# Tiles of an attention and two-MLP kernel made 32 bytes longer, at other places mod 128 bytes

## The chip, the cores and the metric

The kernel runs on one core of one Trainium2 chip. The metric is the time of one execution on the device in microseconds, as the median of the runs.

## The reference

Chunked attention, then an MLP with a product of two projections, then an MLP with a rational function, all in float32:

```python
batch, n_heads, seq, head_dim = (4, 8, 576, 64)      # 2304 tokens, d_model 512
# attention within chunks of 64 tokens
scores = scale * np.matmul(q_c, k_c.transpose(0, 1, 2, 4, 3))
attn = softmax(scores)                                # over the 64 keys of the chunk
x = np.matmul(attn, v_c)                              # -> [2304, 512]
# first MLP, d_ff 1536
a = x @ w_a
b = x @ w_b
y = a * b @ w_out
# second MLP, d_ff 2048
h = y @ w_in
P = a[0] + a[1] * h + a[2] * h2 + a[3] * h3           # h2 = h * h, h3 = h2 * h
Q = 1.0 + np.abs(b[0]) * np.abs(h) + np.abs(b[1]) * h2
out = (P / (Q + 1e-06)) @ w_out2
```

The weights come as float64; the kernel reads them as pairs of 32-bit words.

## The kernel before

Each float32 operand of a product is split into a high and a low part of type float32r, and a product is the sum of three matmuls: high by high, high by low, low by high (`mm3`, lines 252 to 254; for y the same three stand in lines 682, 683 and 685). Every matmul has its own load of weights.

The work runs in stages on TensorE. First, for the first 768 tokens, attention in units of 128 tokens runs interleaved with the projections a and b (`ab_half`). While this goes on, the 24 tiles of w_a and w_b arrive as raw words (`w_fetch`, line 172), are turned into float32 by ScalarE and VectorE in four pieces (`w_piece`) and split (`w_hi`, `w_lo`). Attention of the other 1536 tokens follows the same way, and its result is turned into sums of blocks of x. Second, from some 175 us, a and b of these tokens are made from seven products of such sums in place of eight (`s_product`, `s_step`). Third, from some 354 us, y is made in five blocks of tokens (`y_banks`), while the weights of the second MLP are converted. Fourth, from some 500 us, come h, the rational function and the output, in five blocks of 384, 512, 512, 512 and 384 tokens and 16 steps each (`step2`): `h_part` multiplies w_in by y, `g_front`, `g_back` and `g_split` make the function on ScalarE and VectorE, `o_part` multiplies by w_out2.

The order of the work is written out by hand, as a list for the start, as due times for attention, and as loops for the rest. The loads of q, k, v and the weights are issued by SyncE in this order.

These are the pools that the change touches. All tiles have 128 partitions.

- `p_w`: 12 tiles, w0 to w11, of 4096 bytes per partition. w0 to w7 hold w_a and w_b, high parts in the first half and low parts in the second; w8 to w11 are a ring of four for raw words (`AHEAD`). Later w0 to w11 hold w_out; some of them hold factors of the sums (`ws_`). In the fourth stage w0 to w3 hold y of even blocks, w8 to w11 y of odd blocks (`y_fetch`, one tile for each quarter of d_model), w4 to w6 the temporaries u, t and r (`h_tile`, two halves used in turn), w7 every third pair g_hi and g_lo (`g_split`).
- `p_w2`: 32 tiles, v0 to v31, of 4096 bytes, for w_in (even numbers) and w_out2 (odd numbers). It lies over the memory of the X tiles and others, which are dead by then.
- `p_X`: 14 tiles of 6144 bytes, for the sums of x (`x_block`) and, before that, for k, q and v of the first six units (`a_load`).

Other pools keep their tiles: x of the first tokens (`p_x0`), which later holds factors of the sums (`j_x`), g_hi and g_lo (`p_g`), results on the way to memory (`p_io`), the ring of |h| (`a_ring`). The lengths of all these tiles are multiples of 128 bytes.

Of the kernel before, what the change touches and what calls it, by code (L numbers as in the profile page):

```python
# [9 lines left out]
F32 = mybir.dt.float32  # L10
F32R = mybir.dt.float32r
I32 = mybir.dt.int32
# [8 lines left out]
def chunk_attention_two_mlps(  # L21
# [34 lines left out]
    nc = tc.nc  # L56
    P = 128
    B, H, S, D = q.shape
    NT, DM = out.shape
# [7 lines left out]
    F2 = DFF2 // P  # L67
# [6 lines left out]
    GH = GT // 2  # L74
    UH = GH // P
    NQ = NT // GT
# [9 lines left out]
    AHEAD = 4  # L86
    NWP = 12 - AHEAD
# [5 lines left out]
    START2 = [sum(SIZES2[:j]) for j in range(len(SIZES2))]  # L93
# [6 lines left out]
    p_w = ctx.enter_context(tc.tile_pool(name="w", bufs=1))  # L100
# [8 lines left out]
    y_d = dram.tile([P, KD, NT], F32, name="y_d", tag="y_d")  # L109
# [8 lines left out]
    def split(hi, lo, x):  # L118
        nc.scalar.copy(hi, x)
        nc.vector.tensor_tensor(lo, x, hi.bitcast(F32), ALU.subtract)  # L120
# [4 lines left out]
    p_X = s_X.enter_context(tc.tile_pool(name="X", bufs=1))  # L125
# [22 lines left out]
    w_at = {key: n for n, key in enumerate(order)}  # L148
    w1_d = {k: dram.tile([P, DM], F32, name=f"w_{k[0]}_{k[1]}", tag=f"w_{k[0]}_{k[1]}") for k in order1}

    wt = {}
    raws = {}
    terms = {}
# [4 lines left out]
    def w_fetch():  # L158
        key = order[n_cv[0]]
        at = n_cv[0]  # L160
        n_cv[0] += 1
        if at < len(order1):
            t = p_w.tile([P, DM, 2], I32, name="w_raw", tag=f"w{NWP + at % AHEAD}")
        elif at < len(order1) + len(ordero):
            t = p_x32.tile([P, DM, 2], I32, name="w_raw", tag="x32")
        else:
            t = p_cv.tile([P, DM, 2], I32, name="w_raw", tag="w_raw")
        dst = t.rearrange("p f t -> p (f t)")
        src = w_src[key]
        if len(src.shape) == 3:  # L170
            dst = dst.rearrange("p (k f) -> p k f", k=src.shape[1])
        nc.sync.dma_start(out=dst, in_=src)
        raws[key] = t

    def w_tile(key, dtype):
        at = w_at[key]
        if at < len(order1):
            pool, tag = p_w, f"w{at % NWP}"
        elif at < len(order1) + len(ordero):
            pool, tag = p_w, f"w{at - len(order1)}"  # L180
        else:
            pool, tag = p_w2, f"v{at - len(order1) - len(ordero)}"
        t = pool.tile([P, 2, DM], dtype, name=f"w_{key[0]}_{key[1]}_{at}", tag=tag)
        return t[:, 0], t[:, 1]

    def w_fetch_ahead(n):
        while n_cv[0] < n_cv[2] and n_cv[0] < n + (AHEAD if n_cv[0] < len(order1) else 2):
            w_fetch()

    def w_hi(n):  # L190
        if n in f32s:
            key = order[n]
            wt[key] = w_tile(key, F32R)
            nc.scalar.copy(wt[key][0], f32s[n].bitcast(F32))
# [6 lines left out]
    def w_piece():  # L201
# [5 lines left out]
        if piece == 0:  # L207
            w_fetch_ahead(n)
            t = raws.pop(key)

            terms[n] = (t, *w_tile(key, I32))
# [68 lines left out]
    raw = {}  # L280
    un = {}
# [5 lines left out]
    xs = {}  # L287

    def x_block(g, c):
        if (g, c) not in xs:  # L290
            xs[g, c] = p_X.tile([P, 2, 2, GH], F32R, name="xs", tag=f"X{g}_{c}")
        return xs[g, c]

    def a_tmp(u, name):
# [6 lines left out]
    def a_load(u, *names):  # L301

        (b0, c0), (b1, c1) = divmod(2 * u, NCH), divmod(2 * u + 1, NCH)
        for nm, src in (("k", k), ("q", q), ("v", v)):
            if nm not in names or u >= NU:
                continue
            if u < 2 * UH:
                if ("raw", u) not in un:
                    un["raw", u] = p_X.tile([P, 3, H, D], F32, name="kqv", tag=f"X{NQ - 1}_{u + 1}")
                t = un["raw", u][:, "kqv".index(nm)]  # L310
            else:
                t = p_qk.tile([P, H, D], F32, name=nm, tag=nm, bufs=2 if nm == "v" else 1)
            if b0 == b1:
                parts = [(t, src[b0, :, c0 * CH:(c0 + 2) * CH, :])]
            else:
                parts = [
                    (t[c * CH:(c + 1) * CH], src[bb, :, cc * CH:(cc + 1) * CH, :])
                    for c, (bb, cc) in enumerate(((b0, c0), (b1, c1)))
                ]
            for dst, s in parts:  # L320
                nc.sync.dma_start(out=dst, in_=s.rearrange("h s d -> s h d"))
            raw[nm, u] = t
# [181 lines left out]
    j_x = {}  # L504
    J_AT = {"20": 0, "21": 1, "10": 2, "11": 3, "a1": 4, "b": 5}

    def j_room(nm):

        t, at = divmod(J_AT[nm], 3)
        if ("j", t) not in j_x:  # L510
            j_x["j", t] = p_x0.tile([P, 3, 2, DM], F32R, name="j_x", tag=f"x_{('hi', 'lo')[t]}")
        return j_x["j", t][:, at]
# [8 lines left out]
    def s_prep(i):  # L521


        f = wf.pop(i)
        flat = f.rearrange("p a f -> p (a f)")
        n = 2 * P
        made = {}

        def place(nm):
            if nm == "a" and i % 2 == 0:  # L530
                return p_j2.tile([P, 2, DM], F32R, name="ws_a", tag="ws_a")

            at = {"20": 8, "10": 9, "a1": 10, "b0": 11, "b1": 11}.get(f"{nm}{i}")
            if nm == "b":
                if at not in j_x:
                    t = j_room("b") if at is None else p_w.tile([P, 2, DM], F32R, name="ws_b", tag=f"w{at}")
                    j_x[at] = t.rearrange("p a f -> p (a f)").rearrange("p (i a f) -> p i a f", i=2, a=2)
                return j_x[at][:, i % 2]
            if at:
                return p_w.tile([P, 2, DM], F32R, name="ws_" + nm, tag=f"w{at}")  # L540
            return j_room(f"{nm}{i % 2}")

        def hi(nm, at, m, products):
            def f():
                t = made[nm] = place(nm)[:, :, :m]
                for x, c in enumerate(products):
                    ws[i, c] = t[:, 0, x * n:(x + 1) * n], t[:, 1, x * n:(x + 1) * n]
                nc.scalar.copy(t[:, 0], flat[:, at:at + m])
            return f

        def lo(nm, at, m):
            return lambda: nc.vector.tensor_tensor(
                made[nm][:, 1], flat[:, at:at + m], made[nm][:, 0].bitcast(F32), ALU.subtract
            )

        def add(o, x, y, op):
            return lambda: nc.vector.tensor_tensor(f[:, o], f[:, x], f[:, y], op)

        return [
            hi("a", 0, 2 * n, (1, 2)), hi("b", 3 * n, n, (4,)), lo("a", 0, 2 * n), lo("b", 3 * n, n),  # L560
            add(3, 2, 3, ALU.add), add(2, 0, 2, ALU.subtract), add(0, 3, 0, ALU.subtract),
            hi("2", 2 * n, 2 * n, (7, 5)), add(1, 1, 0, ALU.subtract), hi("1", 0, 2 * n, (6, 3)),
            lo("2", 2 * n, 2 * n), lo("1", 0, 2 * n),
        ]
# [133 lines left out]
    y = {}  # L698

    def y_fetch(j, kk):  # L700


        n = SIZES2[j]
        t = p_w.tile([P, 2, DM], F32R, name="y", tag=f"w{kk if j % 2 == 0 else 8 + kk}")
        y[j, kk] = t[:, 0, :n], t[:, 1, :n]
        nc.sync.dma_start(out=t[:, 1, :n].bitcast(F32), in_=y_d[:, kk, START2[j]:START2[j] + n])

    def y_split(j, kk):
        hi, lo = y[j, kk]
# [13 lines left out]
    h_t = {}  # L723

    def h_tile(nm, n):

        if nm not in h_t:
            at = 4 + "utr".index(nm)
            h_t[nm] = [p_w.tile([P, 2, DM], F32, name=nm, tag=f"w{at}"), 0]
        h_t[nm][1] ^= 1  # L730
        return h_t[nm][0][:, h_t[nm][1], :n]

    def g_front(j, i):

# [20 lines left out]

    def g_split(j, i, t):
        if n_g[0] % 3 == 1:
            w = p_w.tile([P, 2, DM], F32R, name="g_hl", tag="w7")
            hi, lo = (w[:, x, :t.shape[1]] for x in range(2))
        else:  # L760
            hi, lo = (p_g.tile(t.shape, F32R, name=x, tag=x) for x in ("g_hi", "g_lo"))
        n_g[0] += 1
        split(hi, lo, t)
        g2[j, i] = (hi, lo)
# [52 lines left out]
    for item in LOADS:  # L817
        if item == "w":
            w_fetch()
        else:  # L820
            a_load(int(item[1]), item[0])
# [3 lines left out]
    for item in FIRST:  # L825
# [9 lines left out]
        what, u = item[:-1], int(item[-1])  # L835
# [40 lines left out]
    for op in range(12):  # L876
        at = min(END + 2 + 0.5 * (op // 3), 2.0 * len(seq) - 0.5)
# [30 lines left out]
    for t in range(1, F1):  # L908

        if t == 1:  # L910
            at = [(0, m // 2) for m in range(12)]
        elif t == 2:
            at = [(2, m) for m in (3, 3, 4, 5)] + [(3, m) for m in (0, 1, 2, 3, 3, 4, 5, 6)]
        else:
            at = [(2 * t - 2 + m // 6, FILLS[m % 6]) for m in range(12)]
# [19 lines left out]
    for n, (i, g) in enumerate(seq2):  # L935
        place[:] = [n, 0]
        if n == len(seq2) - 1:
# [3 lines left out]
            t = p_x32.tile([P, 2, SIZES[0]], F32, name="g_raw", tag="x32")  # L941
# [98 lines left out]
```

## Time and profile before

| | |
|---|---|
| median of 3 runs | 906.7 us (906.33 to 906.87) |
| profiled execution | 904.24 us |
| its span, first to last instruction | 902.5 us |
| busy: TensorE, its weight loads | 883.7 us (98%), 788.0 us (87%) |
| busy: VectorE, ScalarE, GpSimd | 723.3 us (80%), 612.7 us (68%), 63.9 us (7%) |
| chain that ended last | PE 92%, DVE 4%, ACT 2%, DMA 1% |
| moved by DMA | 105.83 MB |

In the rows, PE is TensorE's matmuls, PEld its weight loads, DVE VectorE, ACT ScalarE, POOL GpSimd and SP SyncE. L252 is line 252. A matmul's row in the timeline has its start and a modelled duration, which overlaps the next one; the spacing is the difference of two starts.

### The profile page before, as it was taken

What the parts mean: (1) busy time and instruction counts of PE and PEld (TensorE: products, weight loads), DVE (VectorE), ACT (ScalarE), POOL (GpSimd) and SP (SyncE); (2) the same over time, 40 slices, a digit from 0 to 9 for tenths busy, and PEclk for the clock granted to TensorE, in tenths of its full rate; (3) what the DMA queues carried; (4) which work ended last, traced back from release to release, by engine and by line L of the source; (5) the groups of instructions that cost most, each with busy time, mean ns of one, the idle gap of its engine ahead of it and who ended that gap; (6) DMA issues with size and microseconds to landing.
All of it is one profiled execution on the core that took longest, in us unless ns stands there. A gap on an engine that the chain in (4) does not pass through costs nothing.

```text
span 902.5 us, 14772 instructions
## 1 busy us (share of the span) xinstructions
PE 883.7 (98%) x5532; PEld 788.0 (87%) x5532; DVE 723.3 (80%) x1321; ACT 612.7 (68%) x1105; POOL 63.9 (7%) x122
## 2 busy tenths in 40 slices
PE   6989999999999999999999999999999999999998
PEld 5879989999999999988888998888888888888987
DVE  5657788497878886578778599998889988988886
ACT  5857888445554553678777688877677667776775
POOL 0111111111111111100000000000000000000000
PEclk9999999999999999999999999999999999999999
DMA  9969886333343423778777200200020002000100
GB/s 233 263 200 263 251 239 171 106 130 126 127 146 123 147 85 105 245 250 277 261 243 256 94 1 1 82 1 1 1 93 1 1 1 82 0 1 1 48 1 36
DMA packets 107336, 105.83 MB, mean 117 GB/s; under 512 B 61440, under 2 KB 84480, under 8 KB 107264
## 3 DMA queue, kind: packets, MB, share of 16 engines
q1 hardware_dynamic: 99264, 79.71, 29.6%
q0 software_dynamic: 8000, 25.17, 7.5%
q8 instruction: 43, 0.70, 0.3%
q14 instruction: 29, 0.24, 0.1%
HBM read 74.98 MB, written 29.88 MB: 116 GB/s over the span
## 4 chain that ended last, share of the span: by engine, by line
PE 92%; DVE 4%; ACT 2%; DMA 1%; issue 0%; SPq 0%; DVEq 0%; ACTq 0%
PE h L254 7%; PE acc L254 7%; PE acc L253 7%; PE h L252 7%; PE h L253 7%; PE acc L252 7%; PE acc L682 5%; PE acc L683 5%; PE acc L685 5%; PE ab L252 3%; PE ab L254 3%; PE ab L253 3%; PE y L253 3%; PE y L254 3%; PE y L252 3%; PE q L252 2%
## 5 line engine op out<-in xcount | busy, mean ns | idle before, releaser
L254 PE MATMUL h<-y,w_i 128*128 128x512 f32 (+1 forms) x320 | 117.8, 368 | 0.0
L252 PE MATMUL h<-y,w_i 128*128 128x512 f32 (+1 forms) x320 | 117.8, 368 | 0.0
L253 PE MATMUL h<-y,w_i 128*128 128x512 f32 (+1 forms) x320 | 117.7, 368 | 0.0
L739 ACT ACTIVATE a_ring<-h 128x512 f32<-128x512 f32 (+1 forms) x80 | 44.1, 551 | 88.0 <-PE h L254 88.0
L580 ACT COPY s<-y 128x384 f32<-128x384 f32 x72 | 34.4, 480 | 80.0 <-PE y L254 79.9
L682 PE MATMUL acc<-g_hi,w_o 128*128 128x512 f32 (+1 forms) x240 | 86.9, 369 | 0.0
L683 PE MATMUL acc<-g_hi,w_o 128*128 128x512 f32 (+1 forms) x240 | 86.8, 368 | 0.0
L742 DVE SCALAR_TENSOR_TENSOR u<-u,cb_t,a_ring 128x512 f32<-128x512 f32 (+1 forms) x80 | 55.7, 696 | 30.2 <-ACT u L740 29.4
L254 PE MATMUL acc<-w_o,g_lo 128*128 128x512 f32 x191 | 74.7, 391 | 0.0
L253 PE MATMUL acc<-w_o,g_hi 128*128 128x512 f32 x191 | 74.6, 391 | 0.0
L252 PE MATMUL acc<-w_o,g_hi 128*128 128x512 f32 x191 | 74.3, 389 | 0.0
L253 PEld LDWEIGHTS h<-y,w_i 128*128 128x128 f32 x320 | 60.1, 188 | 8.8
L252 PEld LDWEIGHTS h<-y,w_i 128*128 128x128 f32 x320 | 60.1, 188 | 8.8
L254 PEld LDWEIGHTS h<-y,w_i 128*128 128x128 f32 x320 | 60.1, 188 | 7.4
L662 DVE TENSOR_TENSOR g_lo<-g_raw,g_hi 128x512 fp32r<-128x512 f32 (+1 forms) x60 | 38.2, 638 | 28.1 <-ACT g_hi L660 15.4
L685 PE MATMUL acc<-g_lo,w_o 128*128 128x512 f32 (+1 forms) x240 | 59.3, 368 | 0.0
L741 ACT ACTIVATE t<-h,ca_t 128x512 f32<-128x512 f32 (+1 forms) x80 | 59.0, 737 | 0.0
L752 DVE SCALAR_TENSOR_TENSOR u<-u,r 128x512 f32<-128x512 f32 (+1 forms) x80 | 50.6, 632 | 9.5 <-ACT r L751 9.5
L744 DVE SCALAR_TENSOR_TENSOR t<-t,ca_t,h 128x512 f32<-128x512 f32 (+1 forms) x80 | 55.6, 695 | 2.8
L751 ACT ACTIVATE r<-r,nlsh 128x512 f32<-128x512 f32 (+1 forms) x80 | 54.5, 682 | 2.6
L750 ACT ACTIVATE r<-u,nlsh 128x512 f32<-128x512 f32 (+1 forms) x80 | 55.6, 695 | 0.3
L753 DVE SCALAR_TENSOR_TENSOR t<-t,ca_t,r 128x512 f32<-128x512 f32 (+1 forms) x80 | 55.4, 692 | 0.0
(195 smaller groups left out, 2400.9 us busy)
## 6 DMA issues: line engine op xcount, KB each, us to landing
w_raw<-in_moe_w_out_dram SPq DMA_DIRECT2D x28, 512.0 KB, 3.9
g_d<-g POOLq DMA_DIRECT2D x72, 192.0 KB, 2.5
g_raw<-g_d SPq DMA_DIRECT2D x48, 256.0 KB, 4.2
w_raw<-in_moe_w_in_dram SPq DMA_DIRECT2D x16, 512.0 KB, 4.6
w_raw<-in_moe_w_a_dram SPq DMA_DIRECT2D x12, 512.0 KB, 4.8
w_raw<-in_moe_w_b_dram SPq DMA_DIRECT2D x12, 512.0 KB, 5.2
out_dram<-o SPq DMA_DIRECT2D x18, 256.0 KB, 2.4
y_d<-ys POOLq DMA_DIRECT2D x16, 256.0 KB, 4.1
```

The lines of the kernel that those rows point to most:

```text
L252: nc.tensor.matmul(ps, wh, xh, start=first, stop=False, **kw)
L253: nc.tensor.matmul(ps, wh, xl, start=False, stop=False, **kw)
L254: nc.tensor.matmul(ps, wl, xh, start=False, stop=last, **kw)
L682: nc.tensor.matmul(acc[j][d], wh, gh, start=i == 0, stop=False)
L683: nc.tensor.matmul(acc[j][d], wl, gh, start=False, stop=False)
L685: nc.tensor.matmul(acc[j][d], cols(w, d)[0], gl, start=False, stop=i == F1 - 1)
L741: nc.scalar.activation(t, ps, AF.Identity, scale=ca_t[:, 3:4], bias=ca_t[:, 2:3])
L742: nc.vector.scalar_tensor_tensor(u, u, cb_t[:, 0:1], ah, ALU.add, ALU.mult)
L744: nc.vector.scalar_tensor_tensor(t, t, ca_t[:, 1:2], ps, ALU.add, ALU.mult)
L750: nc.scalar.activation(r, u, AF.Ln, scale=2.0 ** -LSH, bias=nlsh[:, 0:1])
L751: nc.scalar.activation(r, r, AF.Exp, scale=-1.0, bias=nlsh[:, 1:2])
L753: nc.vector.scalar_tensor_tensor(t, t, ca_t[:, 0:1], r, ALU.add, ALU.mult)
```

## The change

A helper `room` makes the tiles of the three pools 8 elements (32 bytes) longer, and hands out a part that begins 0, 4 or 8 elements (0, 16 or 32 bytes) into the tile. Tags are numbered: w0 to w11 are 0 to 11, v0 to v31 are 12 to 43, X tags get numbers from 44 on in the order of their first use. w6 to w11 begin 16 bytes in, w0 to w5 at 0. From number 12 on, four tags in a row begin at 0, the next four at 16, the next four at 32 bytes, and so on. The users of these tiles take them as flat rows and shape them themselves; what they read and write is otherwise the same.

```diff
+    def room(pool, tag, dtype, name, size=2 * DM):
+        n = rooms.setdefault(tag, len(rooms))
+        t = pool.tile([P, size + 8], dtype, name=name, tag=tag)
+        return t[:, 4 * (n > 5 if n < 12 else (n - 12) // 4 % 3):][:, :size]
+
+    rooms = {f"w{n}": n for n in range(12)}
+    rooms.update({f"v{n}": 12 + n for n in range(2 * F2)})
...
-            t = p_w.tile([P, DM, 2], I32, name="w_raw", tag=f"w{NWP + at % AHEAD}")
+            t = room(p_w, f"w{NWP + at % AHEAD}", I32, "w_raw").rearrange("p (f t) -> p f t", t=2)
...
-        t = pool.tile([P, 2, DM], dtype, name=f"w_{key[0]}_{key[1]}_{at}", tag=tag)
-        return t[:, 0], t[:, 1]
+        t = room(pool, tag, dtype, f"w_{key[0]}_{key[1]}_{at}")
+        return t[:, :DM], t[:, DM:]
...
-            xs[g, c] = p_X.tile([P, 2, 2, GH], F32R, name="xs", tag=f"X{g}_{c}")
+            t = room(p_X, f"X{g}_{c}", F32R, "xs", 4 * GH)
+            xs[g, c] = t.rearrange("p (a b f) -> p a b f", a=2, b=2)
...
-                    un["raw", u] = p_X.tile([P, 3, H, D], F32, name="kqv", tag=f"X{NQ - 1}_{u + 1}")
+                    t = room(p_X, f"X{NQ - 1}_{u + 1}", F32, "kqv", 4 * GH)
+                    un["raw", u] = t.rearrange("p (a h d) -> p a h d", a=3, h=H)
...
-                return p_w.tile([P, 2, DM], F32R, name="ws_" + nm, tag=f"w{at}")
+                return room(p_w, f"w{at}", F32R, "ws_" + nm).rearrange("p (a f) -> p a f", a=2)
...
-        t = p_w.tile([P, 2, DM], F32R, name="y", tag=f"w{kk if j % 2 == 0 else 8 + kk}")
-        y[j, kk] = t[:, 0, :n], t[:, 1, :n]
+        t = room(p_w, f"w{kk if j % 2 == 0 else 8 + kk}", F32R, "y")
+        y[j, kk] = t[:, :n], t[:, DM:DM + n]
...
-            h_t[nm] = [p_w.tile([P, 2, DM], F32, name=nm, tag=f"w{at}"), 0]
+            h_t[nm] = [room(p_w, f"w{at}", F32, nm), 0]
         h_t[nm][1] ^= 1
-        return h_t[nm][0][:, h_t[nm][1], :n]
+        return h_t[nm][0][:, h_t[nm][1] * DM:][:, :n]
...
-            w = p_w.tile([P, 2, DM], F32R, name="g_hl", tag="w7")
-            hi, lo = (w[:, x, :t.shape[1]] for x in range(2))
+            w = room(p_w, "w7", F32R, "g_hl")
+            hi, lo = (w[:, x * DM:][:, :t.shape[1]] for x in range(2))
```

The factor b of the sums (`ws_b`) in w11 goes through `room` in the same way.

## Rows read from the trace of the kernel before

**Rows 1.** The page: engines, chain by engine, DMA issues (KB, median us to landing).

```profile
PE 883.7 (98%) x5532; PEld 788.0 (87%) x5532; DVE 723.3 (80%) x1321; ACT 612.7 (68%) x1105; POOL 63.9 (7%) x122
...
PE 92%; DVE 4%; ACT 2%; DMA 1%; issue 0%; SPq 0%; DVEq 0%; ACTq 0%
...
w_raw<-in_moe_w_out_dram SPq DMA_DIRECT2D x28, 512.0 KB, 3.9
```

**Rows 2.** Stretches: from:to us, busy us (x count) of each engine, clock, DMA share, GB/s.

```profile
0.00:25.00 25.00, 16.59 (x250) 14.59 (x253) 15.29 (x39) 15.84 (x29) 1.91 (x8) 1.00 0.96 234
25.00:50.00 25.00, 20.92 (x250) 18.13 (x246) 17.90 (x43) 18.39 (x35) 3.88 (x7) 1.00 1.01 265
50.00:75.00 25.00, 23.47 (x298) 21.12 (x288) 14.84 (x35) 15.67 (x33) 3.77 (x7) 1.00 0.73 224
...
175.00:350.00 175.00, 175.00 (x1011) 174.68 (x1010) 141.34 (x276) 89.24 (x172) 25.05 (x46) 1.00 0.36 124
...
575.00:800.00 225.00, 225.00 (x994) 186.29 (x994) 200.24 (x304) 164.85 (x272) 0.00 (x0) 1.00 0.08 26
...
875.00:902.50 27.50, 23.56 (x115) 20.46 (x113) 19.00 (x36) 16.20 (x32) 0.00 (x0) 1.00 0.08 30
```

**Rows 3.** Timeline of PE, start and us: runs of 512, 384 and 256 columns.

```profile
699.72 0.39 PE L253 MATMUL h<-y,w_i 128*128 128x512 f32 x1
...
700.63 0.39 PE L254 MATMUL h<-y,w_i 128*128 128x512 f32 x1
...
224.84 0.33 PE L252 MATMUL q<-xs,j_x 128*128 128x384 f32 x1
...
225.36 0.33 PE L252 MATMUL q<-xs,j_x 128*128 128x384 f32 x1
...
371.68 0.28 PE L682 MATMUL acc<-g_hi,w_o 128*128 128x256 f32 x1
...
372.28 0.28 PE L683 MATMUL acc<-g_hi,w_o 128*128 128x256 f32 x1
```

**Rows 4.** Timeline of PE in a block of 384: first h matmuls, then the output's.

```profile
530.68 0.33 PE L252 MATMUL h<-y,w_i 128*128 128x384 f32 x1
...
531.75 0.33 PE L252 MATMUL h<-y,w_i 128*128 128x384 f32 x1
...
532.79 0.39 PE L252 MATMUL acc<-w_o,g_hi 128*128 128x512 f32 x1
...
534.87 0.33 PE L252 MATMUL h<-y,w_i 128*128 128x384 f32 x1
```

**Rows 5.** Single lines: count, duration ns min/median/max, first and last start.

```profile
L252 PEld LDWEIGHTS h<-y,w_i x320: 187/188/188, 500.5 to 889.5; 128*128 128x128 f32 x160
...
L743 DVE TENSOR_TENSOR t<-h,t x41: 682/689/692, 578.5 to 795.4; 128x512 f32<-128x512 f32 x41
...
L119 ACT CAST g_hi<-t x28: 622/627/627, 578.3 to 795.3; 128x512 fp32r<-128x512 f32 x28
...
L194 ACT CAST w_a<-w_x x12: 614/623/655, 16.0 to 157.0; 128x512 fp32r<-128x512 f32 x12
```

**Rows 6.** Chain of the head; DMA issues 25 to 50 us; tiles that change owner.

```profile
2.79 5.96 DMA kqv<-in_k_dram
...
23.97 6.14 DMA w_raw<-in_moe_w_a_dram
30.13 0.79 ACT w_a L217
...
w_raw<-in_moe_w_b_dram SPq DMA_DIRECT2D x4, 512.0 KB, 7.8
w_raw<-in_moe_w_a_dram SPq DMA_DIRECT2D x3, 512.0 KB, 8.8
...
L254 PE MATMUL q<-xs,j_x x32: 334/334/346, 301.1 to 356.2; 128*128 128x384 f32 x32
...
L221 DVE TENSOR_SCALAR w_i<-w_raw x16: 418/422/427, 366.3 to 485.7; 128x512 f32<-128x512 f32 x16
```

More of the change, by code (lines that the diff above doesn't have):

```diff
@@ L535, in place @@
                 if at not in j_x:
-                    t = j_room("b") if at is None else p_w.tile([P, 2, DM], F32R, name="ws_b", tag=f"w{at}")
-                    j_x[at] = t.rearrange("p a f -> p (a f)").rearrange("p (i a f) -> p i a f", i=2, a=2)
+                    if at is None:
+                        t = j_room("b").rearrange("p a f -> p (a f)")
+                    else:
+                        t = room(p_w, f"w{at}", F32R, "ws_b")
+                    j_x[at] = t.rearrange("p (i a f) -> p i a f", i=2, a=2)
                 return j_x[at][:, i % 2]
             if at:
-                return p_w.tile([P, 2, DM], F32R, name="ws_" + nm, tag=f"w{at}")
+                return room(p_w, f"w{at}", F32R, "ws_" + nm).rearrange("p (a f) -> p a f", a=2)
             return j_room(f"{nm}{i % 2}")
@@ L703, in y_fetch @@
         n = SIZES2[j]
-        t = p_w.tile([P, 2, DM], F32R, name="y", tag=f"w{kk if j % 2 == 0 else 8 + kk}")
-        y[j, kk] = t[:, 0, :n], t[:, 1, :n]
-        nc.sync.dma_start(out=t[:, 1, :n].bitcast(F32), in_=y_d[:, kk, START2[j]:START2[j] + n])
+        t = room(p_w, f"w{kk if j % 2 == 0 else 8 + kk}", F32R, "y")
+        y[j, kk] = t[:, :n], t[:, DM:DM + n]
+        nc.sync.dma_start(out=y[j, kk][1].bitcast(F32), in_=y_d[:, kk, START2[j]:START2[j] + n])
     def y_split(j, kk):
```

## The prediction

> **What bounds the kernel now.** I read the busy shares first. TensorE (PE) is busy 98% of the span, its weight loads (PEld) 87%, VectorE (DVE) 80%, ScalarE (ACT) 68%, and the chain that ended last consists of PE for 92% [rows 1]. The table by stretch then says where PE has no room left [rows 2]: in the stretches from 175 to 350 us and 575 to 800 us it is busy for every microsecond, at a granted clock of 1.00. Only the first 75 us (14.0 us idle) and the tail (3.9 us idle) leave anything. So an edit of operand places can move the time in three ways: the spacing of matmuls changes, the head changes, or the tail does.
>
> The spacing is read from the starts in the timeline. Four spacings of 512 columns take 0.91 us, three of 384 columns 0.52 us, five of 256 columns 0.60 us [rows 3]: 227, 173 and 120 ns. From 256 to 512 columns that is 107 ns more, 0.417 ns a column, the 2.4 GHz level. What is left over is 13.3 ns at each of the three sizes. The stretches confirm it over long times: 175 us hold 1011 matmuls, nearly all of 384 columns, and 225 us hold 994 of 512 [rows 2], 173 and 226 ns each.
>
> One irregularity exists. Where blocks of y have 384 columns, matmuls of 384 and of 512 columns alternate. There the first six of 384 take from 530.68 to 531.75, 178 ns each; the nine of 512 take from 532.79 to 534.87, 231 ns each [rows 4]. That is 0.03 and 0.04 us more than at the steady spacing, 0.07 us in a step; 32 steps (two blocks of 16) make 2.2 us.
>
> **The change part by part.** No instruction is added, removed or moved. DMAs keep their sizes, queues and order. Per partition, tiles w0 to w11, v0 to v31 and the X tiles become 32 bytes longer; each next tile of a pool then begins 32 bytes further mod 128. Before, every length in these pools is a multiple of 128 bytes, so all tiles of a pool begin at one place.
>
> *Matmul spacing.* The matmuls of lines 252 to 254 and 682 to 685 number 4128 by the loops (576 of the first product, 1008 of its sums, 720 for y, 960 for h, 864 for the output). Their 13.3 ns make 4128 x 13.3 ns = 55 us. This is the end of what could be saved, if those 13.3 ns were a collision of the moving rows and the weights, both being read from one place mod 128. I take 0, for three reasons in rows. First, the remainder is the same at 256, 384 and 512 columns and for tiles of different pools [rows 3]. Second, weight loads last 187 to 188 ns in all 320 of the h group [rows 5], without a sign of a read that sometimes meets another. Third, DVE and ACT read and write the same memory 89% and 73% of the time from 575 to 800 us [rows 2], at whatever phase they happen to have, and the matmul spacing doesn't answer. If operands at one place mod 128 hindered each other, some of these streams should show it. The 2.2 us of the irregularity is the part of the spacing that does vary; it follows a change of size, not of tile, so I leave it too, but it is the likeliest small gain. The other end is a loss: a spacing as uneven everywhere as behind a change of size, 4.4 ns (231 less 226.7) on each of 4128 matmuls, 18 us.
>
> *VectorE and ScalarE.* Line 743 on DVE, which works in place on a temporary, lasts 682 to 692 ns in 41 instances; ACT's cast of line 119 from t into g_hi lasts 622 to 627 ns [rows 5]. There is no spread here to win back. Where DMAs are dense, ACT's cast of line 194 spreads from 614 to 655 ns around 623 [rows 5], 5% at most. PE hides all of that from 75 us on. In the head, up to 50 us, the chain has 26 pieces of ACT, some 14 us; the one behind the w_raw wait is among the longer [rows 6]. 5% of them is 0.7 us either way; I take 0.
>
> *DMA.* Tiles w8 to w11 begin at 16, 48, 80 and 112 mod 128 afterwards, and w_raw of the first 24 weight tiles lands there. The kqv loads land in X tiles that keep multiples of 32. The chain shows that this matters in the head alone: 5.96 us on the first k load and 6.14 us on a w_raw load [rows 6], while the DMA engines are busy at a share of 0.96 and 1.01 [rows 2]. No row shows a landing at 16 bytes off. The nearest are loads of the same 512 KB in the same 25 us, which land in a median of 7.8 and 8.8 us [rows 6]: 1.0 us apart with nothing different in place. I take 0, since that row lies closest to what is moved. The end on the slow side: seven such loads stand in those 25 us [rows 6], some 14 in the first 50, through a ring of four tiles; 1.0 us a turn makes 14 / 4 x 1.0 = 3.5 us. The end on the fast side is the chain's load landing like the quiet ones of w_out, 3.9 us [rows 1] in place of 6.14: 2.2 us less.
> The page "DMA: Bandwidth & Descriptors" of the Trainium skill, section How a descriptor splits into AXI transactions, says that a transfer is cut at 256-byte boundaries into beats of 32 bytes and that an unaligned start costs extra beats; no run here shows it yet. By that page, an estimate: a piece of 1 KB has 32 beats and gets from one to eight more by where it begins; four more on the 7.3 MB of those loads, over half of what moves in 50 us, would be 3.7 us.
>
> *Waits for reused memory.* The v tiles lie over dead X, sum and load tiles. Their borders move by up to 1.4 KB, so a first write may have to wait for another old tile. The sums of x are read last at 356.2 us; the first piece of w_in writes at 366.3 us [rows 6]. The cover is 10 us; cost 0. Were it gone, DVE and ACT would start a piece later, and PE needs w_in only from 500 us.
>
> Sum: 0 + 0 + 0 + 0. The profiled execution took 904.24 us, of which the span is 902.5 us and 1.7 us lie around it; the median of the runs is 906.7 us, 2.5 us above. A sum of zero keeps both: 906.7 us.
>
> **The rivals.**
> (A) The 13.3 ns are a collision, and the new places undo it. For it: a remainder of the same size stands on every matmul, PE reads moving rows and the next weights at once, and the remainder isn't rigid behind a change of size [rows 4]. Against it, the three reasons above. The price follows from the places: after the change, h's weights (v0, v2, ...) and y still coincide in 10 of 64 pairs for even blocks and 6 of 64 for odd ones, about one in eight, so seven eighths of 55 us go: 48 us, 858.6 us.
> Here the skill's pages speak on both sides. "TensorE: Matmul & The Clock Gate" of the Trainium skill, section Back-to-back issue gap, has 2.5 ns over the columns for a warm matmul, where this trace has 13.3; by the page, an estimate, 4128 x 10.8 ns = 45 us of this kernel isn't the array's. "SBUF — State Buffer" of the Trainium skill, section Who interferes with whom, says that PE and ACT never wait on anyone, which is against the change.
> (B) Only small things gain: the irregularity goes, 2.2 us: 904.5 us. For it, the irregularity varies while all else is steady; against it, it looks the same for different tiles.
> (C) Slower: raw loads at 16 bytes off take longer. It happens in the first 50 us, where the DMA share is 1 and ACT waits for a w_raw at 24 us [rows 6]. It decides as soon as a load takes longer than the slack of the ring, and there is none in that stretch: 3.5 us, 910.2 us. Behind 75 us PE covers it.
> (D) New collisions: reads that kept out of each other's way meet now. 18 us: 925 us. The same rows speak against it as against A.
> If the allocator rounded the padding away, the time would be 906.7 us too; that counts with the forecast.
>
> **How the numbers follow.** Nothing that can be measured: 0.52. A 0.10, B 0.15, C 0.15, D 0.08. What a measurement can tell from no change is about 0.2%, 1.8 us; B and C lie just beyond it. So faster is 0.25, same 0.52, slower 0.23. The range takes in the forecast, B and C with the bounds of the head: down by 2.2 + 0.7 + 2.2 = 5.1 us to 901.6, rounded to 901; up by 3.5 + 0.7 us to 910.9, and with a few of D's matmuls (1.1 of its 18 us) to 912. A and D are left out, 0.18.
>
> **What would show it.** In the profile after: starts of matmuls at 512, 384 and 256 columns 227, 173 and 120 ns apart if I am right; 215 to 220, 162 to 165 and 108 to 112 if A is. Where a pair still coincides (the weights in v0 with y in w0) beside one that doesn't, A would show two spacings in one block. B shows where blocks of 384 run: the 178 and 231 ns of now would be 173 and 227. C shows in the landing of w_raw and in the idle time before 75 us, D in starts that are uneven where they are even now. I am wrong if any steady spacing moves by 1 ns: that alone is 4 us. The weakest step is that one, since no tile of before lies at another place than its neighbours.

## The result, and the profile after

| | before | after |
|---|---|---|
| median of the runs | 906.52 us (903.71 to 906.87, 4 runs) | 917.38 us (914.83 to 918.79, 4 runs) |
| profiled execution, its span | 904.24 us, 902.5 us | 916.12 us, 914.3 us |
| ratio | | 1.0124, 95% interval 1.0090 to 1.0157 |

The changed kernel is 1.24% slower, 10.9 us by the medians and 11.8 us by the two spans. The forecast of 906.7 us was wrong, and so was its range: 917.38 us lies 5.4 us above its upper end.

In the changed kernel lines 252 to 254 are 260 to 262, and 682, 683 and 685 are 695, 696 and 698. The page of the changed kernel: engines, the chain that ended last, two groups of matmuls (busy us, mean ns | idle before).

```profile
PE 894.6 (98%) x5532; PEld 789.7 (86%) x5532; DVE 723.6 (79%) x1321; ACT 612.7 (67%) x1105; POOL 64.2 (7%) x122
...
PE 93%; DVE 3%; ACT 2%; DMA 1%; SPq 1%; issue 0%; DVEq 0%; ACTq 0%
...
L260 PE MATMUL h<-y,w_i 128*128 128x512 f32 (+1 forms) x320 | 118.7, 371 | 0.0
...
L695 PE MATMUL acc<-g_hi,w_o 128*128 128x512 f32 (+1 forms) x240 | 87.8, 372 | 1.0 <-ACT g_hi L673 1.0
```

The same 5532 matmuls keep PE busy 10.9 us longer (894.6 against 883.7 in [rows 1]). DVE has 0.3 us more, ACT the same 612.7 us. So the time is on PE, and hardly in waits: the matmuls of h had no idle time in front of them, those of y 1.0 us.

The table by stretch (us, then busy us and count for each engine, granted clock, DMA share, GB/s), first of the changed kernel, then two rows of the kernel before that [rows 2] don't hold:

```profile
0.00:75.00 75.00, 60.86 (x767) 53.25 (x768) 47.73 (x113) 49.41 (x94) 9.60 (x22) 0.95 0.92 240
...
175.00:350.00 175.00, 175.00 (x1003) 174.86 (x1002) 140.39 (x274) 88.53 (x170) 25.12 (x46) 1.00 0.37 125
350.00:375.00 25.00, 23.90 (x179) 23.43 (x178) 14.11 (x31) 9.83 (x21) 2.17 (x4) 1.00 0.45 147
375.00:500.00 125.00, 125.00 (x543) 101.30 (x543) 94.12 (x173) 92.71 (x158) 8.95 (x16) 1.00 0.76 259
...
575.00:800.00 225.00, 225.00 (x974) 182.41 (x973) 196.50 (x298) 161.89 (x268) 0.00 (x0) 1.00 0.08 26
```

```profile
350.00:375.00 25.00, 24.93 (x183) 24.10 (x182) 14.98 (x32) 10.99 (x25) 2.70 (x5) 1.00 0.53 176
375.00:500.00 125.00, 125.00 (x553) 103.52 (x552) 94.47 (x173) 92.38 (x157) 8.23 (x15) 1.00 0.76 255
```

PE is busy for the whole of 575 to 800 us in both, at a granted clock of 1.00, but gets 974 matmuls done in place of 994 [rows 2]; from 375 to 500 us 543 in place of 553; from 175 to 350 us 1003 in place of 1011. The 20 lost ones are worth 20/974 x 225 = 4.6 us, the 10 are worth 2.3 us, the 8 worth 1.4 us: 8.3 us of 11.8 in three stretches, and the last stage goes on beyond 800 us. The head shows nothing of the kind: 767 matmuls and 60.9 us of PE in its 75 us, where the kernel before has 769 and 61.0 us, though the granted clock there was 0.95 in this execution and 1.00 before.

The timeline of PE in the changed kernel, 512 columns, nine spacings apart:

```profile
699.54 0.39 PE L260 MATMUL acc<-w_o,g_hi 128*128 128x512 f32 x1
...
701.64 0.39 PE L260 MATMUL h<-y,w_i 128*128 128x512 f32 x1
```

2.10 us for nine are 233 ns each, where 227 stood before [rows 3]. I took all starts of the products' matmuls from the trace and averaged the spacing by stage. "Sums" is 180 to 350 us (384 columns; a few longer gaps are in its averages), "y" 376 to 499 us, "h" and "output" 576 to 800 us (512 columns):

| ns | sums | y | h | output |
|---|---|---|---|---|
| before | 173.6 | 226.7 | 226.7 | 226.7 |
| after | 174.9 | 232.2 | 231.5 | 231.7 |

The steady spacing of before is (columns + 32) / 2.4 GHz. What lies over it adds up to 0.25 us in the sums, nothing in y and 2.0 us from 500 us on (384 and 512 columns) before, and to 1.5, 2.9 and 8.2 us after: 10.3 us more. The rest of the 11.8 us is small: one wait of 1.0 us of the first block of y for its g_hi near 350 us (in the page's row of L695, and in PE's busy time from 350 to 375 us), and some 0.4 us in the first product. That wait isn't the change's: the kernels below that are as fast as the one before have it too (1.2 us with 256 bytes, 1.0 us with the raw loads off).

### The profile page after: what moved, and what is told of

The parts are those of the page before. It is cut to its first block, busy times and chain, and to the rows that moved or that the text cites. A ratio compares the mean times of both kernels' runs of the same rounds, so it can differ in the third digit from the quotient of the medians.

```text
span 914.3 us, 14772 instructions
## 1 busy us (share of the span) xinstructions
PE 894.6 (98%) x5532; PEld 789.7 (86%) x5532; DVE 723.6 (79%) x1321; ACT 612.7 (67%) x1105; POOL 64.2 (7%) x122
## 4 chain that ended last, share of the span: by engine, by line
PE 93%; DVE 3%; ACT 2%; DMA 1%; SPq 1%; issue 0%; DVEq 0%; ACTq 0%
PE h L260 7%; PE h L261 7%; PE acc L260 7%; PE h L262 7%; PE acc L262 7%; PE acc L261 7%; PE acc L695 5%; PE acc L698 5%; PE acc L696 5%; PE ab L260 3%; PE ab L261 3%; PE ab L262 3%; PE y L261 3%; PE y L260 3%; PE y L262 3%; PE q L260 2%
## 5 line engine op out<-in xcount | busy, mean ns | idle before, releaser
L695 PE MATMUL acc<-g_hi,w_o 128*128 128x512 f32 (+1 forms) x240 | 87.8, 372 | 1.0 <-ACT g_hi L673 1.0
```

The costliest lines, as they stand in the source:

```text
L695: nc.tensor.matmul(acc[j][d], wh, gh, start=i == 0, stop=False)
```

## The experiments

Theory 1: the pace of matmuls follows from the distance of the weights being loaded from the rows being read, modulo some number of bytes; before, it supposes, every pair lies at distance 0. Its rivals: the variety of places from tile to tile does it (theory 2 of the first expectations); a place off a border of 128 bytes is slow by itself (theory 3); the traffic of other engines or the raw loads at 16 bytes off do it. "Distance" is, per partition, the place of the weights less that of the rows.

### One step of 32 or 64 bytes between pools

`pad_l`, an unused tile ahead of these pools, is made longer, which moves the w, v and X tiles together against all other pools; nothing else changes.

```diff
-    const.tile([P, 24], F32, name="pad_l", tag="pad_l")
+    const.tile([P, 32], F32, name="pad_l", tag="pad_l")
```

> Kernel before, with one unused tile at the start 32 bytes longer: w, v and X tiles all begin at 32 mod 128, the other pools (g_hi, g_lo, x of the first tokens, j_x) stay at 0. Nothing varies from tile to tile. Theory 1 (the place of the weights against the moving rows counts): y's stage, 375 to 500 us, has weights at 32 and rows at 0 and goes from 227 to about 233 ns; the output's matmuls and the first product too, the sums by 2 ns; h (both at 32) stays at 227 where it isn't behind a change. Some 10 to 13 us more than before, about 918 us. Theory 2 (it is the variety of places, since each change of tile throws the pace out as a change of size does): 906.7 us, all spacings 227 and 173 ns. Theory 3 (the place mod 128 itself counts): h gets slower as well, 920 us and more.

> As the one before, 64 bytes in place of 32. Theory 1 has two forms: if places count mod 64, as the changed kernel's trace suggests (mean spacing of 512-column matmuls 225.7 + 4.2 ns over columns both at a distance of 0 and of 64, 6 ns more at the others), this is 906.7 us with 227 ns in y's stage; if they count mod 128, about 918 us again. Theory 2: 906.7 us. Theory 3: over 910 us.

 (40 in place of 32)

Measured: 915.24 us at 32 bytes, ratio 1.0097 (1.0071 to 1.0124); 910.72 us at 64 bytes, ratio 1.0048 (1.0029 to 1.0067). The table by stretch, at 32 bytes and then at 64:

```profile
175.00:350.00 175.00, 175.00 (x995) 174.87 (x994) 139.20 (x271) 88.27 (x170) 24.55 (x45) 1.00 0.36 125
375.00:500.00 125.00, 125.00 (x548) 101.13 (x547) 94.22 (x175) 93.76 (x160) 8.90 (x16) 1.00 0.77 259
```

```profile
175.00:350.00 175.00, 175.00 (x1010) 174.80 (x1009) 140.61 (x274) 88.85 (x172) 25.08 (x46) 1.00 0.37 127
375.00:500.00 125.00, 125.00 (x545) 101.03 (x544) 94.50 (x175) 93.68 (x159) 8.89 (x16) 1.00 0.77 259
```

Spacings: at 32 bytes 176.4 ns (sums), 233.3 (y), 227.1 (h), 230.7 (output); at 64 bytes 173.6, 233.3, 226.6, 228.2. The rows from 375 us begin with up to 3 us of matmuls of 256 columns in this and the next kernels, so the spacings say more than the counts. h, whose weights (v tiles) and rows (w tiles) moved together, stays at its pace; where weights and rows moved apart, the sums, y and the output lose it at 32 bytes, y and the output at 64. That is theory 1, and against a place that is slow by itself. It isn't the variety of places either, since nothing here varies from tile to tile. One step between two pools costs nearly as much as the whole change, 9.5 of 10.9 us. A period of 64 bytes falls with the second kernel, whose 910.72 us neither form of theory 1 had expected (906.7 or 918).

The output holds a contrast within one stage. Its rows (w_out2) are in v tiles; of its weights, two thirds are in `p_g`, which stayed, and one third in w7 (g_hl), which moved with the rows. At 32 bytes, nine spacings of each:

```profile
688.61 0.39 PE L252 MATMUL acc<-w_o,g_hl 128*128 128x512 f32 x1
...
690.65 0.39 PE L252 MATMUL acc<-w_o,g_hl 128*128 128x512 f32 x1
...
694.06 0.39 PE L252 MATMUL acc<-w_o,g_hi 128*128 128x512 f32 x1
...
696.16 0.40 PE L252 MATMUL acc<-w_o,g_hi 128*128 128x512 f32 x1
```

They are 227 and 233 ns. By the starts from 576 to 800 us, the pairs that moved together have 226.7 ns at 32 and at 64 bytes, those that moved apart 232.7 and 229.0 ns.

### 128 and 256 bytes

> Kernel before, with the unused tile at the start 128 bytes longer: w, v and X tiles begin 128 bytes further than the other pools' tiles, and all tiles lie at 0 mod 128 as before. If the distance counts mod 128, as the change supposes: 906 us and 227 ns in y's stage. If it counts over a longer period, as the run of matmuls alone hints (233 ns at a distance of 128, 227 at 256): about 233 ns in y's stage and 911 to 916 us. Variety of places would say 906 us.

 (56 elements)

> As the one before with 256 bytes. If the distance counts and its period divides 256: 906 us, 227 ns in y's stage, 173 ns in the sums, like the kernel before, though every tile of three pools lies elsewhere. If not: 910 us and more.

 (88 elements)

Measured: 917.61 us at 128 bytes, ratio 1.0122 (1.0101 to 1.0142); 905.70 us at 256 bytes, ratio 0.9997 (0.9984 to 1.0010). At 128 and then at 256 bytes:

```profile
375.00:500.00 125.00, 125.00 (x547) 101.64 (x546) 94.92 (x175) 93.88 (x159) 8.85 (x16) 1.00 0.77 259
...
575.00:800.00 225.00, 225.00 (x980) 184.00 (x980) 197.93 (x300) 163.49 (x271) 0.00 (x0) 1.00 0.08 26
```

```profile
375.00:500.00 125.00, 125.00 (x554) 103.50 (x553) 94.28 (x172) 93.23 (x160) 8.77 (x16) 1.00 0.77 260
575.00:800.00 225.00, 225.00 (x994) 186.31 (x993) 200.22 (x304) 165.97 (x274) 0.00 (x0) 1.00 0.08 26
```

At 128 bytes every tile still begins at 0 mod 128, and the kernel is as slow as the changed one (spacings 175.9, 232.4, 228.8, 231.0 ns), a little slower than expected. At 256 bytes all four spacings are those of before. The period is 256 bytes, and beginning on a border of 128 bytes doesn't help. One number doesn't fit: h at 128 bytes has 228.8 ns, though its rows and weights moved together. The first seven of its twelve matmuls behind the output's are uneven, and then 227 ns is back; at 32 and 64 bytes it was there at once. Why is open.

### Matmuls alone

Three kernels of nothing but matmuls, all from the same two tiles, one for the rows and one for the weights; each run of matmuls reads both at places of its own.

```python
for r in range(count):
    m, s = places[r % len(places)]        # bytes: rows at m, weights at s
    nc.tensor.matmul(ps[:, :n], sta[:, s // 4:s // 4 + P], mov[:, m // 4:m // 4 + n], start=r == 0, stop=r == count - 1)
```

> No attention and no MLP: long runs of 40 matmuls alone, with the next weights and the moving rows at chosen places, nothing else running; its time is that of these runs. Theory 1: 512 columns at a distance of 0 (and 128, 256, 512, 1024 bytes) 226.7 ns, at 64 bytes the same or near, at 16, 32, 48, 80, 96 and 112 about 231 to 234 ns; moving rows and weights shifted together 226.7 ns. 384 columns: 173.3 at 0 and 64, 175 to 176 at the others. Theory 2: 226.7 and 173.3 ns in every run behind its first ten matmuls. Theory 3: rows and weights shifted together are slow too.

> Matmuls alone again, without attention and MLPs: each run of 36 at a chosen distance of weights and rows follows 16 at a distance of 0, so that all start from the same state. Theory of the distance with a long period: 226.7 ns at 0, 256 and 512 bytes and about 233 at 128 and 384; if it is the state left by the run before that counts, distances that came out slow in the first run of this kind come out at 226.7 here. With high and low parts in turn as in the kernels: the same as with one pair. 256 columns: 120 ns at 0, and perhaps 1 or 2 ns less elsewhere, as the one run at 32 bytes had 118.

> Matmuls alone, as before each run behind 16 at a distance of 0: further distances, two distances in turn, and places that move together. Distance over 256 bytes: 512 columns 229 to 235 ns at 72 to 208 bytes; moved together, 226.7 again after at most ten uneven matmuls; two places in turn at a distance of 0 each: if each jump of place throws the pace out, uneven all the time though the distance is 0, else 226.7. 256 columns: 113.3 ns around 64 and 192 bytes (second run of this kind), 115 to 120 between. A combination below 226 ns at 512 or below 173 at 384 columns, if there is one, would give a kernel faster than before.

Measured: 328.00, 571.33 and 471.51 us. The timeline of the second kernel; a row is a run of matmuls, with its start, its length in us and, in the name, its columns (c512), the rows' place (m) and the weights' place (s):

```profile
31.97 3.80 PE L67 MATMUL c512x_m0B_s0B<-mov,sta 128*128 128x512 f32 x16
35.61 8.56 PE L67 MATMUL c512x_m0B_s32B<-mov,sta 128*128 128x512 f32 x36
44.00 3.80 PE L67 MATMUL c512x_m0B_s0B<-mov,sta 128*128 128x512 f32 x16
...
59.66 8.56 PE L67 MATMUL c512x_m0B_s64B<-mov,sta 128*128 128x512 f32 x36
...
83.80 8.53 PE L67 MATMUL c512x_m0B_s128B<-mov,sta 128*128 128x512 f32 x36
...
107.86 8.40 PE L67 MATMUL c512x_m0B_s192B<-mov,sta 128*128 128x512 f32 x36
...
143.54 8.32 PE L67 MATMUL c512x_m0B_s256B<-mov,sta 128*128 128x512 f32 x36
...
155.33 8.56 PE L67 MATMUL c512x_m0B_s320B<-mov,sta 128*128 128x512 f32 x36
...
286.65 8.42 PE L67 MATMUL c512x_m64B_s0B<-mov,sta 128*128 128x512 f32 x36
...
507.46 4.42 PE L67 MATMUL c256x_m0B_s32B<-mov,sta 128*128 128x256 f32 x36
...
513.64 4.26 PE L67 MATMUL c256x_m0B_s64B<-mov,sta 128*128 128x256 f32 x36
```

From 35.61 to 44.00 us are 36 matmuls at distance 32: 233 ns each. The next run, at distance 0 again, begins at 44.00. Equal lengths show the period: 8.56 at 64 and at 320 bytes; 8.32 at 256, as at distance 0; 8.40 at 192 is nearly 8.42 for rows 64 bytes up, the same distance. Settled spacings of the three kernels (from the starts, without the first 14 of a run), with the weights moved and, from 32 bytes on, also with the rows moved:

| distance, bytes | 0, 256, 512, 1024 | 16, 144, 240 | 4 | 8 | 20, 32 to 72 | 80 | 96 | 128 | 112, 160, 224 | 176 | 192 | 208 |
|---|---|---|---|---|---|---|---|---|---|---|---|
| 512 columns, ns | 226.7 | 226.7 | 232.3 | 230.6 | 233.2 to 233.5 | 232.1 | 234.3 | 232.4 to 233.5 | 233.3 | 230.3 | 228.9 | 232.0 |

The distance isn't all. Rows moved by 16 bytes (distance 240) have 231.4 and 231.8 ns and rows moved by 240 bytes (distance 16) 233.3, where weights moved to the same distances have 226.7. Rows and weights both 16 bytes up, at distance 0, have 233.3 ns in the first kernel and 230.0 in the second; weights 12 bytes up 229.8 and 226.7. So within 16 bytes of a place mod 256 the places themselves, or what ran before, count as well; which of them stays open. The expectations had none of this, and the first had taken 64 bytes for a distance near 226.7.

With 384 columns about half of the distances have 173.3 ns, the others 175.6 to 177.2 (80, 128, 144, 160, 208, 224, 240; 64 either way). With 256 columns it is the other way round: 120.0 at distance 0, less at nearly every other, 113.3 at 64 and 192. No other engine is at work here, so none is needed for it. The numbers carry over: y with its weights 32 or 64 bytes off has 233.3 ns in the kernels, 233.4 and 233.2 to 233.5 here; 128 bytes off 232.4 there, 232.4 and 233.5 here. In the output, rows 64 bytes up (distance 192) have 229.0 ns there and 228.9 here. With 384 columns, distance 192 has 173.3 ns here, as the sums kept 173.6 at 64 bytes.

The third kernel moved weights and rows together in the middle of the stream. Three of its rows:

```profile
202.97 5.63 PE L71 MATMUL c512x_m32B_s32B<-mov,sta 128*128 128x512 f32 x24
...
230.31 5.60 PE L71 MATMUL c512x_m256B_s256B<-mov,sta 128*128 128x512 f32 x24
...
239.37 8.52 PE L71 MATMUL c512x_m0B_s0B_m32B_s32B<-mov,sta 128*128 128x512 f32 x36
```

A move of both by 32 bytes costs 0.03 us (5.63 against 5.60), spread over up to a dozen matmuls, and then 226.7 ns is back. But these two places in turn, each at distance 0, never settled in 36 matmuls: 231.8 ns (8.52 us, against 8.32); 64 bytes apart it is 231.6, 128 bytes apart 228.2. Places 2048 bytes apart in turn stay at 226.7 (second kernel). So a jump of place can count by itself. The changed kernel, whose tiles jump every few matmuls, has both, other distances and jumps; how its 10.9 us divide between them no run here separates.

### The change for v alone, and for w alone

`room` returns the tile as it was for all tags but v0 to v31, or for all but w0 to w11:

```diff
+        if tag[0] != "v":
+            return pool.tile([P, size], dtype, name=name, tag=tag)
```

> One part of the change alone: the tiles v0 to v31 of w_in and w_out2 are 32 bytes longer and begin at 0, 16 or 32 bytes; w and X tiles as in the kernel before. Theory of the distance: stages up to 500 us keep 173 and 227 ns, the last stage has 230 to 232 ns at 512 columns; the trace of the changed kernel has 8.2 us of uneven spacing from 500 us on against 2.0 us before, so about 6 us more than before. Variety of places: the same, which this run doesn't tell apart. Loads at 16 bytes off: no change, as v tiles take no loads.

> The other part alone: w0 to w11 are 32 bytes longer, w6 to w11 used from 16 bytes on; v and X tiles as long as before, all at one place. Distance of weights and rows: y's stage near 232 ns as in the changed kernel (2.9 us there), the last stage near 231 to 232 ns although the v tiles don't vary, since y is in w tiles (some 5 to 6 us), the sums near 173.6; in all 8 to 10 us, 914 to 916 us. With the 7 us of the v tiles alone that is more than the whole change, because the distance in the last stage counts once, whichever of the two is moved.

Measured: v alone 913.09 us, ratio 1.0070 (1.0051 to 1.0090); w alone 916.98 us, ratio 1.0110 (1.0093 to 1.0127). The tables by stretch, v alone first:

```profile
375.00:500.00 125.00, 125.00 (x553) 103.53 (x552) 94.28 (x172) 93.28 (x160) 8.77 (x16) 1.00 0.77 259
575.00:800.00 225.00, 225.00 (x970) 181.93 (x970) 195.78 (x296) 161.87 (x267) 0.00 (x0) 1.00 0.08 26
```

```profile
375.00:500.00 125.00, 125.00 (x551) 101.67 (x551) 94.69 (x175) 94.41 (x160) 8.81 (x16) 1.00 0.77 259
575.00:800.00 225.00, 225.00 (x974) 182.56 (x973) 196.91 (x299) 162.55 (x268) 0.00 (x0) 1.00 0.08 26
```

v alone leaves y at 226.7 ns and the sums at 173.6, and takes h to 232.2 and the output to 232.5: the cost stands where the v tiles are read. w alone costs in every stage (176.0, 232.1, 231.8, 231.5 ns); the first 2.6 us of its row from 375 us are matmuls of 256 columns, so the count of 551 hides it. Its sums were expected near 173.6. But twelve tiles 32 bytes longer are 384 bytes, 128 mod 256, and by the order of the pools X and v tiles move by that against the other pools; 128 bytes gave 175.9 above. So this kernel moves more than the w tiles, which would explain the sums and why it is a little over the expected 914 to 916 us. The parts aren't additive, 0.70% and 1.10% against 1.24% for both: in the last stage each alone has 231.5 to 232.5 ns already, and both together no more.

### Only the raw loads at 16 bytes off

w8 to w11 are 256 bytes longer, and only w_raw begins 16 bytes in; everything that PE reads keeps its place mod 256.

```diff
+        if tag in ("w8", "w9", "w10", "w11"):
+            t = pool.tile([P, size + 64], dtype, name=name, tag=tag)
+            return t[:, 4 * (name == "w_raw"):][:, :size]
```

> Kernel before, with w8 to w11 256 bytes longer and used from the start, but the raw words of the first 24 weight tiles land 16 bytes into them. No matmul's operand moves mod 256. If loads at 16 bytes off take longer: up to 3.5 us more than before and longer landings of w_raw than 4.8 and 5.2 us. If only distances of matmul operands count: 906 us.

Measured: 905.76 us beside 906.95, ratio 0.9985 (0.9973 to 0.9997), all spacings as before. The page's rows of the loads (KB, median us to landing), with them off and then of the kernel before:

```profile
w_raw<-in_moe_w_a_dram SPq DMA_DIRECT2D x12, 512.0 KB, 4.8
w_raw<-in_moe_w_b_dram SPq DMA_DIRECT2D x12, 512.0 KB, 5.0
```

```profile
w_raw<-in_moe_w_a_dram SPq DMA_DIRECT2D x12, 512.0 KB, 4.8
w_raw<-in_moe_w_b_dram SPq DMA_DIRECT2D x12, 512.0 KB, 5.2
```

Loads at 16 bytes off cost nothing; in the changed kernel they take 4.7 and 5.0 us. Rival C falls, and with it my estimate of 3.7 us by the page "DMA: Bandwidth & Descriptors" of the Trainium skill, section How a descriptor splits into AXI transactions: the extra beats, if there are any, don't show in a landing. The page speaks of bytes that are fetched and not used; what moved here is the side that is written, so this says nothing against the page.

### A version that could gain: the first block of y at 64 bytes

The matmuls alone had one thing to offer, 113.3 ns for 256 columns. Only y's first block has that size (144 matmuls).

```diff
-        hi = p_g.tile([P, SIZES[j]], F32R, name="g_hi", tag="g_hi")
+        off = 16 if j == 0 else 0
+        hi = p_g.tile([P, SIZES[j] + off], F32R, name="g_hi", tag="g_hi")[:, off:]
```

g_lo likewise.

> The kernel before, but g_hi and g_lo of the first block of y (144 matmuls of 256 columns) begin 64 bytes into their tiles, so that the weights of those matmuls lie 192 bytes (mod 256) from the rows; everything else is at distance 0 as before. Theory 1 (the distance sets the pace, mod 256 bytes): those matmuls start 113.3 ns apart in place of 120.0, as the matmuls of 256 columns alone did at 64 and 192; 144 x 6.7 ns = 1.0 us less, 905.5 to 906 us beside 906.5 for the kernel before, ratio 0.9989, and the stretch from the first of these matmuls to the first of 512 columns shortens by about 0.9 us. Theory 2 (120 ns is a fixed cost of a matmul of 256 columns in this kernel, and only matmuls without other work beside them can go faster): 120.0 ns as before and the same time.

Measured: 905.76 us beside 906.23 (12 and 17 runs), ratio 0.9995 (0.9987 to 1.0004). Two rows of its timeline, 36 matmuls apart:

```profile
372.25 0.28 PE L683 MATMUL acc<-g_hi,w_o 128*128 128x256 f32 x1
...
376.49 0.40 PE L683 MATMUL acc<-g_hi,w_o 128*128 128x512 f32 x1
```

4.24 us for 36 are 117.8 ns, against 120 before [rows 3]. The direction was right, the size a third: 144 x 2.2 ns = 0.3 us, which no timing of this kernel can show. The last kernel asked why.

> This kernel computes nothing of the reference: it runs matmuls of 256 columns alone, each with its own load of weights, in runs of 48 with rows or weights 64 or 192 bytes off; between them 16 at distance 0. In runs named one, weights and rows stay at one place; in hl, the weights change between two places 2048 bytes apart; in cols, weights and rows go through the places of a step of the first block of y (four columns of high and low weights, then the rows' low part); 1 or 4 is the number of accumulators in turn. It asks why the first block of y went to 118 ns and not to 113.3. Theory 1a (the other places of weights and rows, 512 and 2048 bytes apart, throw the pace out each time although the distance mod 256 stays): one and hl at 113.3, cols at about 118. Theory 1b (the accumulators in turn): 113.3 with 1, 118 with 4. Theory 1c (rows off and weights at 0 isn't the same as weights off and rows at 0): 118 at m64_s0 in all of them, 113.3 at m0_s64 and m0_s192. Theory 2 (it is the other work in the kernel): 113.3 in all. cols4_m0_s0, as in the kernel before, stays at 120.

Its timeline shows four runs of 48 matmuls, whose places (rows, weights) are (64, 0), (192, 0), (0, 64) and (0, 192) in this order:

```profile
25.69 5.82 PE L71 MATMUL c_one_m_s<-mov,sta 128*128 128x256 f32 x48
...
33.27 5.62 PE L71 MATMUL c_one_m_s<-mov,sta 128*128 128x256 f32 x48
...
40.62 5.82 PE L71 MATMUL c_one_m_s<-mov,sta 128*128 128x256 f32 x48
...
48.20 5.60 PE L71 MATMUL c_one_m_s<-mov,sta 128*128 128x256 f32 x48
```

5.82 us are 117.8 ns settled, 5.60 and 5.62 are 113.3. The same four values came back with other places of the same kind and with four accumulators in turn, so 1a and 1b fall; matmuls alone have 117.8 too, so theory 2 falls as well. y's place, (64, 0), has 117.8 here as there. 1c holds for that place, but not as it was put: (192, 0), whose rows are off too, has 113.3, and (0, 64) has 117.8 here and had 113.3 in the second kernel, where the 16 matmuls ahead of it had not settled. One distance can thus have two settled paces; whether the history decides or the place itself as well stays open. Rows at 192 bytes were not tried in the kernel: the 0.7 us more couldn't be timed.

The kernel with 64 bytes between the pools had the place (0, 64) in its first block of y, and there the kernel does reach 113.3 ns. Two of its rows, twelve matmuls apart:

```profile
373.72 0.28 PE L682 MATMUL acc<-g_hi,w_o 128*128 128x256 f32 x1
...
375.08 0.28 PE L682 MATMUL acc<-g_hi,w_o 128*128 128x256 f32 x1
```

1.36 us for twelve are 113.3 ns. So the other work of the kernel doesn't forbid that pace. In the same block the granted clock was 0.50, the 1.2 GHz level, from 369.2 to 372.2 us, after PE had waited 1.8 us for g_hi and started again at 367.89. There the matmuls start 213.3 ns apart, which is 256 / 1.2 GHz with nothing left over: in this block the remainder stood at the higher level alone.

## Why the prediction was wrong

*What bounds the kernel* held. PE alone sets the time from 175 us on, so each nanosecond of spacing came through: 10.3 of 11.8 us.

*Matmul spacing: 0* is the step that failed. Its two ends were -55 and +18 us, and the mechanism of the second came: unevenness as behind a change of size, nearly everywhere. The three reasons that I gave for 0 failed like this. The first, one remainder of 13.3 ns at three sizes and in several pools [rows 3], was constancy without a contrast: all those rows behave as one distance, 0 mod 256, so they couldn't say what another distance does. The prediction says that no tile of before lies at another place than its neighbours, and still took the constancy as evidence. The second, weight loads of 187 to 188 ns [rows 5], is true and says nothing: they are 187 to 192 ns in the changed kernel, and its matmuls are uneven all the same. The third was that DVE and ACT leave no mark on PE. They don't. But the matmuls alone pay with nothing else running, so the cost lies with PE's own operands, the rows and the next weights; that two reads collide there is my reading, and no run shows how. What should have counted was the one place where the pace does vary [rows 4]: it shows that the pace is a state that settles and can be thrown out.

*Rival D* named this and was given 0.08. Its price, 4.4 ns on each of 4128 matmuls, was off in its terms. On 512 columns the mean excess is larger, 5.5 ns in y and 5.1 ns after it, on about 2000 matmuls: 10.4 us, of which 9.2 are new. On the 1008 of the sums it is 1.3 ns more than before, and in the first product's 576 hardly any, 0.4 us in all. So 10.9 us came, not 18. A matmul of 384 columns was counted like one of 512; matmuls alone show that about half of the distances leave it at 173.3 ns.

*Rival A*, the saving, has no row. Among all distances tried none has less than 226.7 or 173.3 ns for 512 or 384 columns, so distance 0 was already the best. It would have been right in one small place that I didn't separate, 256 columns: there 13.3 ns fell to 11 with the rows at 64 bytes and to 6.7 with the weights there, in a kernel as in the matmuls alone. The figure from "TensorE: Matmul & The Clock Gate" (section Back-to-back issue gap) of the Trainium skill, 2.5 ns over the columns, is what that page gives for an isolated warm matmul, and the prediction set it against a stream; at the 2.4 GHz level no run here meets it, the lowest remainder is 6.7 ns. "SBUF — State Buffer" (section Who interferes with whom) calls PE's two reads independent; the runs agree that other engines don't slow PE (226.7 ns beside busy VectorE and ScalarE, 226.7 alone), and not on the two reads, which cost up to 7.6 ns more by their distance alone (234.3 less 226.7).

*Rival B* didn't come: 9 spacings of 512 columns behind 384 stay at 231 ns in the changed kernel, and the even ones joined them.

*VectorE and ScalarE, DMA, waits for memory: 0* held. Busy times moved by 0.3 and 0.0 us, loads at 16 bytes off land in the same time, and no wait for memory under w_in shows. The slow bound of the loads was a little large: 12 of them, not some 14, are issued in the first 50 us of the kernel before, which makes 3.0 us and not 3.5. The 1.0 us wait near 350 us varies from one execution to the next, as said above.

*The period.* I reckoned mod 128, as the change is put; the runs say mod 256. My count of pairs that still coincide (10 and 6 of 64) has no meaning.

## What to carry to other kernels

A row that is the same everywhere is evidence only against causes that differ somewhere in it; before taking 0 for an edit, ask whether the trace holds one instance of the state that the edit makes. Where PE is the bound and each matmul loads its own weights, keep weights and rows at one place mod 256 bytes in all pools, and treat an odd length allocated ahead of them as a change of the inner loop: 32 bytes cost this kernel 1%. A few dozen matmuls alone, at the places in question, agree with the kernel within 0.2 ns at 32 and 64 bytes and 512 columns. At 128 bytes one run was 1.1 ns off, and for y's first block they foretold 113.3 ns where 117.8 came: they had moved the weights, the kernel moved the rows.

## What the hardware showed that I had not expected

- The spacing of matmuls with a weight load each depends on the distance of the weights from the rows mod 256 bytes: 226.7 to 234.3 ns at 512 columns, 173.3 to 177.2 at 384, 113.3 to 120.0 at 256. Near 0 it also matters which of the two is moved: distance 16 had 226.7 ns by the weights and 233.3 by the rows.
- The 13.3 ns over columns / 2.4 GHz is no fixed cost: 6.7 ns at 256 columns and 64 bytes, 21 ns at 512 columns and 96 bytes, and nothing over columns / 1.2 GHz in the one stretch at a granted clock of 0.50 (213.3 ns at 256 columns).
- The pace is a state. A jump of size or place is followed by up to a dozen uneven matmuls (0.03 us); two places 32 bytes apart in turn don't settle (231.8 ns); one distance had several paces, 226.7 ns at distance 0 with both 32 bytes up and 233.3 and 230.0 with both 16 up, 117.8 and 113.3 at distance 64 with 256 columns.
- A DMA that lands 16 bytes off in each partition took no longer (4.8 and 5.0 us against 4.8 and 5.2).
